# Loads split and placed one by one, an extra weight slot, the last inner blocks taken output by output, and one operand's differences on another engine

## The chip, the cores and the metric

The kernel runs on one core of a Trainium2 chip, in one launch. Times are device microseconds (us) of that core. Three timed runs of the kernel before gave 666.07, 663.64 and 663.92 us, median 663.92 us. Below, TensorE is PE in the rows (PEld is its weight load), VectorE is DVE, ScalarE is ACT, GpSimd is POOL, and SyncE's DMA queue is SP or SPq.

## The reference

Three stages follow each other: attention with a pooled part and a local part, a first MLP with a gate, and a second MLP of four experts, weighted by shares.

```
# attention, 2 batches, 8 heads, 576 tokens, 64 per head
q_d, k_d, v_d = (mean over groups of 4 tokens of q, k, v)
out_d = softmax(q_d k_d^T / 8) v_d            # repeated 4 times: out_up
scores = q k^T / 8, kept where |i - j| < 4
out_local = softmax(scores) v
x = out_up + out_local                         # 1152 tokens x 512
# first MLP
h = x @ w_in                                   # 512 -> 2048
g = h * clip(h + 3, 0, 6) / 6
x = g @ w_out                                  # 2048 -> 512
# second MLP
p = domain_probs / sum(domain_probs)
for e in range(4):
    out += p[:, e] * (relu(x @ w1[e]) @ w2[e]) # 512 -> 1024 -> 512
```

## The kernel before

**Attention** runs over eight units (a batch and a pair of heads), numbered by `t` in the loop at line 969. In its turn a unit gets its pooled scores, its mask and its local scores on TensorE, and the softmax on VectorE, ScalarE and GpSimd. In the same turn the unit before it is transposed (L627), and the one two back gets its values (L717, L728). All engines but SyncE keep the order in which the code is written; the queue of loads on SyncE is ordered by a scheduler, which puts a load as early as its slot allows. To hold a load to a place in the program, the code writes one element of its target on VectorE first (L171, L404): the load then comes behind that write. The keys and queries of units 6 and 7 (`load_qk(3)`), the first w_in block (`load_to(0)`) and the values of the second batch (`load_v(1, ..)`) are loaded in turns 1 to 3.

**First MLP.** w_in and w_out come as eight blocks each of 64-bit floats; each is loaded into one slot and turned into a high and a low float by `converting()`, a generator of steps on ScalarE and VectorE (L221, L231, L245, L254, L205, L210). Each product is three matmuls: high by high, high by low, low by high (`three`, L360 to L362). `first` computes h by 16 inner blocks `f` and three token chunks `c`; the gate is written at L790. After each, `convert(1)` takes a step if more than two slots are unused. The second half multiplies the gates by w_out: for each chunk it runs over 16 inner blocks and for each block over four outputs `dt`, with four banks (`accs`) open; after the last block ScalarE copies them to `x2` (L863). A slot is given back by `done_with`.

**Second MLP.** Each `r` is half an expert. The products with w1 use a scheme of seven block products in place of eight, and for it x is kept in two halves of 576 tokens, each as seven blocks: four own and the differences T1 to T4, high and low of each. `blocks_of_x2` makes them: GpSimd subtracts (`sub2`, L284), ScalarE writes the high part (L290) and VectorE the low (L295). Half 0 is made during the last chunk of the first MLP; half 1 in the first `r` (`xop1`), while TensorE works on half 0. A `Unit2` is one quarter of the inner size by one half of the tokens: `open`, `middle` and `close` are 12, 18 and 12 matmuls (L875), with sums on VectorE (L415, called `u` and `c`), Relu on ScalarE (L904) and the low part on VectorE (L907). In the first `r` the first two units need half 0 alone. From line 1134 on VectorE, ScalarE and GpSimd keep the order of the code. The shares are computed ahead of the loop (L1142 to L1147), from a load of 18 KB.

Of the kernel before, what the change touches and what calls it, by code (L numbers as in the profile page):

```python
# [82 lines left out]


# [29 lines left out]
def model(ctx: ExitStack, tc: tile.TileContext, qT, kT, v, dp, w_in, w_out, w1, w2, out):  # L114
# [60 lines left out]
    def converting():  # L175
# [42 lines left out]
        for i in range(2 * NW):  # L218
# [23 lines left out]
            elif i == 0:  # L242
                load_to(1)
# [123 lines left out]
    def load_qk(pair, units=(0, 1)):  # L367

        b, hp = divmod(2 * pair + units[0], NHP)
        if pair not in k_slots:  # L370
            k_slots[pair], q_slots[pair] = take(), take()
        n = len(units)
        at = units[0]
        k, q = k_slots[pair][0], q_slots[pair][0]
        k = k[:, at * SK : (at + n) * SK].rearrange("p (u s) -> p u s", u=n)
        for edge in (slice(0, FACTOR - 1), slice(SK - FACTOR + 1, SK)):
            nc.gpsimd.memset(k[:, :, edge], 0.0)
        nc.sync.dma_start(out=k[:, :, FACTOR - 1 : FACTOR - 1 + S], in_=kT[b, :, hp : hp + n])
        q = q[:, at * S : (at + n) * S].rearrange("p (u s c) -> p s u c", u=n, s=2)
        for s in range(2):  # L380
            nc.sync.dma_start(out=q[:, s], in_=qT[b, s, :, hp : hp + n, :])

# [10 lines left out]
    def load_v(b, p):  # L393
        v_slots.setdefault(b, []).append(take())
        slot, o = v_slots[b][p][0], FACTOR - 1
        if p == 0:
            nc.vector.memset(slot[:o, :DM], 0.0)
            v_rows(b, p, o, 0, WR, 0, 1)
            v_rows(b, p, WP, WP - o, WP, 0, 1)
            v_rows(b, p, 0, QB - o, P, 1, 2)  # L400
            v_rows(b, p, 0, 4 * QB - o, P, 2, 4)
        elif p == 1:
            if b:
                nc.vector.memset(slot[:1, :1], 0.0)  # L404
            v_rows(b, p, 0, 8 * QB - o, P, 0, 2)
            v_rows(b, p, 0, 12 * QB - o, P, 2, 4)
# [51 lines left out]
    load_qk(0, (0,))  # L458
    load_qk(0, (1,))
# [334 lines left out]
    def split_gate(c, f):  # L794
        g = hp_.tile([P, 2, TC], F32R, tag="h", name="h", bufs=NF2)
# [21 lines left out]
    def blocks_of_x2(s, x):  # L817

# [5 lines left out]
        room = x2_pair(s, 0)[:, 2 * PAIR : 3 * PAIR].rearrange("p (k n) -> p k n", k=2)  # L824
# [410 lines left out]
```

## Time and profile before

| | |
|---|---|
| timed runs, median | 663.92 us (663.64 to 666.07) |
| profiled execution, own time | 666.61 us |
| its span, first to last instruction | 664.9 us |
| mean granted TensorE clock | 0.992 |
| TensorE busy | 649.1 us (98%) |
| VectorE, ScalarE, GpSimd busy | 416.6, 253.6, 102.1 us |
| the chain that ended last | TensorE 89%, VectorE 6%, DMA 2% |

Read it so: TensorE is the engine with almost no idle time, and the chain of work that ended last lies on it. The rest is in three places that the 40 slices of the page show: slices 2 and 3 (from 16.6 us), slice 13 (from 199 us) and slice 18 (from 282 us). In the first and the last of them the granted clock is below full, too. VectorE is full in slices 5 to 7, 11 and 12.

### The profile page before, as it was taken

How to read it: one execution, taken by the hardware profiler on the slowest of the kernel's cores; microseconds unless marked ns; L12 is line 12 of the kernel's file. 1: busy time of each engine (PE TensorE's matmuls, PEld its weight loads, DVE VectorE, ACT ScalarE, POOL GpSimd, SP SyncE). 2: the span in 40 equal slices, each digit the busy share in tenths (PEclk: the TensorE clock that was granted, in tenths of full speed). 3: DMA queues.
4: the chain of work that ended last, by engine and by line, in shares of the span. 5: the costliest groups of instructions: out<-in, count | busy, mean ns of one | idle time of the engine just before them, and what ended most of it. 6: DMA issues, size and time to landing. Idle time of an engine off the chain costs nothing.

```text
span 664.9 us, 11951 instructions
## 1 busy us (share of the span) xinstructions
PE 649.1 (98%) x4929; PEld 584.3 (88%) x4943; DVE 416.6 (63%) x825; ACT 253.6 (38%) x591; POOL 102.1 (15%) x146
## 2 busy tenths in 40 slices
PE   7989999999999999989999999999999999999997
PEld 3556899999998999988898898898998998988985
DVE  5556799942598229296575575565665665765742
ACT  5536676542475236243133142233232241331310
POOL 4653100000000034060120211201201201201000
PEclk9979999999999999989999999999999999999999
DMA  8825233300350013200120110110110210300012
GB/s 279 278 69 190 82 111 127 127 1 0 127 191 1 0 64 102 90 1 1 38 90 0 64 65 1 63 64 1 65 64 0 68 61 0 123 5 1 1 48 96
DMA packets 11859, 45.89 MB, mean 69 GB/s; under 512 B 1302, under 2 KB 3350, under 8 KB 7708
## 3 DMA queue, kind: packets, MB, share of 16 engines
q1 hardware_dynamic: 11804, 45.12, 20.0%
q8 instruction: 39, 0.64, 0.4%
q14 instruction: 16, 0.13, 0.1%
HBM read 42.76 MB, written 2.36 MB: 68 GB/s over the span
## 4 chain that ended last, share of the span: by engine, by line
PE 89%; DVE 6%; DMA 2%; issue 1%; POOL 1%; SPq 1%; ACT 0%; POOLq 0%
PE bank L875 26%; PE bank L1120 10%; PE bank L1122 10%; PE bank L1121 10%; PE bank L362 9%; PE bank L360 8%; PE bank L361 8%; PE pair L717 2%; PE pair L524 2%; DVE slot L231 1%; PE pair L728 1%; DMA slot<-in_v_dram 1%; DMA slot<-in_qT_dram 1%; DVE slot L210 1%; DVE slot L254 1%
## 5 line engine op out<-in xcount | busy, mean ns | idle before, releaser
L875 PEld LDWEIGHTS bank<-xop,slot 128*128 128x128 f32 x1344 | 182.2, 189 | 3.8 <-DVE u L415 2.5
L875 PE MATMUL bank<-xop,slot 128*128 128x288 f32 x1344 | 183.5, 296 | 2.0 <-DVE u L415 2.0
L1120 PE MATMUL bank<-slot,h 128*128 128x512 f32 x288 | 113.5, 394 | 0.0
L1122 PE MATMUL bank<-slot,h 128*128 128x512 f32 x288 | 113.0, 392 | 0.0
L1121 PE MATMUL bank<-slot,h 128*128 128x512 f32 x288 | 111.9, 389 | 0.0
L1128 DVE SCALAR_TENSOR_TENSOR slot<-bank,pr,slot 128x512 f32<-128x512 f32 x63 | 47.3, 751 | 82.5 <-PE bank L1122 82.5
L415 POOL TENSOR_TENSOR st<-slot 128x256 f32<-128x256 f32 x16 | 13.2, 824 | 444.4 <-DMA slot<-in_w_dram 247.6
L362 PE MATMUL bank<-h,slot 128*128 128x384 f32 x192 | 65.0, 338 | 0.9 <-DVE slot L210 0.9
L360 PE MATMUL bank<-h,slot 128*128 128x384 f32 x192 | 64.9, 338 | 0.5 <-ACT slot L205 0.5
L1122 PEld LDWEIGHTS bank<-slot,h 128*128 128x128 f32 x288 | 54.1, 188 | 12.6
L361 PE MATMUL bank<-h,slot 128*128 128x384 f32 x192 | 64.7, 337 | 0.0
L1121 PEld LDWEIGHTS bank<-slot,h 128*128 128x128 f32 x288 | 54.1, 188 | 11.5
L1120 PEld LDWEIGHTS bank<-slot,h 128*128 128x128 f32 x288 | 54.1, 188 | 10.3
L360 PE MATMUL bank<-x,slot 128*128 128x384 f32 x188 | 63.1, 336 | 0.0
L362 PE MATMUL bank<-x,slot 128*128 128x384 f32 x188 | 62.9, 335 | 0.0
L361 PE MATMUL bank<-x,slot 128*128 128x384 f32 x188 | 62.9, 335 | 0.0
L415 DVE TENSOR_TENSOR u<-bank,u 128x288 f32<-128x288 f32 x96 | 43.5, 453 | 21.4 <-PE bank L875 21.1
L904 ACT ACTIVATE h<-c 128x288 fp32r<-128x288 f32 x64 | 27.9, 445 | 73.4 <-DVE c L415 73.3
L790 DVE SCALAR_TENSOR_TENSOR slot<-t,bank 128x384 f32<-128x384 f32 x47 | 25.8, 551 | 28.7 <-ACT t L789 28.4
L789 ACT ACTIVATE t<-bank,half__145 128x384 f32<-128x384 f32 x47 | 27.1, 581 | 41.9 <-PE bank L362 41.9
L290 ACT ACTIVATE slot<-st 128x512 fp32r<-128x512 f32 x32 | 19.2, 624 | 62.1 <-POOL st L284 62.1
L798 DVE TENSOR_TENSOR h<-slot,h 128x384 fp32r<-128x384 f32 x48 | 27.5, 582 | 22.2 <-ACT h L797 22.2
(115 smaller groups left out, 930.8 us busy)
## 6 DMA issues: line engine op xcount, KB each, us to landing
slot<-in_w_dram SPq DMA_DIRECT2D x16, 1024.0 KB, 4.8
slot<-in_w_in_dram SPq DMA_DIRECT2D x8, 1024.0 KB, 4.9
slot<-in_w_out_dram SPq DMA_DIRECT2D x8, 1024.0 KB, 4.8
slot<-in_v_dram SPq DMA_DIRECT2D x6, 512.0 KB, 9.3
out_dram<-slot SPq DMA_DIRECT2D x9, 256.0 KB, 2.0
slot<-in_kT_dram SPq DMA_DIRECT2D x3, 576.0 KB, 3.9
slot<-in_qT_dram SPq DMA_DIRECT2D x6, 288.0 KB, 5.5
slot<-in_kT_dram SPq DMA_DIRECT2D x2, 288.0 KB, 4.1
```

Source lines behind the costliest of these rows:

```text
L360: nc.tensor.matmul(ps, wh, xh, start=first, stop=False)
L361: nc.tensor.matmul(ps, wh, xl, start=False, stop=False)
L362: nc.tensor.matmul(ps, wl, xh, start=False, stop=last)
L415: eng.tensor_tensor(out=out, in0=a, in1=b, op=ALU.add)
L789: nc.scalar.activation(out=t, in_=ps, func=AF.Relu, bias=half_, scale=1.0 / (6.0 * UP))
L798: nc.vector.tensor_tensor(out=g[:, 1, :], in0=u, in1=r32(g[:, 0, :]), op=ALU.subtract)
L875: nc.tensor.matmul(ps, a[:, i, k], b[:, j, k], start=start and k == 0 and n == 0, stop=stop and k == 1 and n == 2, skip_group_check=True,)
L904: nc.scalar.activation(out=self.h[:, 0, i, j], in_=of, func=AF.Relu)
L1120: nc.tensor.matmul(ps, hh, w[:, 0], start=(f == 0), stop=False)
L1121: nc.tensor.matmul(ps, hh, w[:, 1], start=False, stop=False)
L1122: nc.tensor.matmul(ps, hl, w[:, 0], start=False, stop=(f == NF - 1))
L1128: nc.vector.scalar_tensor_tensor(out=to, in0=ps, scalar=share, in1=to, op0=ALU.mult, op1=ALU.add)
```

## The change

- **Loads of attention.** `load_next(t)` is called three times in every turn from 2 on, and each call issues one entry of the list `later`: the first w_in block in two halves, the values of batch 1 in four pieces, keys and queries of the last pair apart, the second w_in block in two halves. Most have a write of one element on VectorE ahead (`hold`). The steps of conversion begin in turn 3, with two.
- **First MLP.** A pool `late` with one more slot of weight size, from the end of attention on; the pool of split gates `h` has 7 buffers in place of 8; from inner block 11 on a step is taken if more than one slot is unused, in place of two.
- **Last inner blocks.** For the last chunk the last three blocks run output by output: for each `dt` all three blocks, then ScalarE's copy of that output.
- **Half 1 of x.** Its differences are six subtractions of 128x288 and one of twice that on VectorE, the first six ahead of the loop; high and low parts are spread over the first three units. The shares move behind the third unit.

```diff
+NL = 1
+NH = 7
+AHEAD = 2
+LAST = 3
...
-    SHORT = ("more", "slots", "mlp1")
-    LONG, FIRST = ("mlp1", "slots"), ("slots", "mlp1")
+    SHORT = ("more", "slots", "late", "mlp1")
+    LONG, FIRST = ("late", "mlp1", "slots"), ("slots", "late", "mlp1")
...
-            if i < 2:
-                nc.vector.memset(raw[i][0][:1, :1], 0.0)
             nc.sync.dma_start(out=raw[i][0].bitcast(I32), in_=sources[i])
...
+    def hold(part):
+
+        nc.vector.memset(part[:1, :1], 0.0)
+
+    def load_half(i, h):
+        if h == 0:
+            raw[i] = take(order=SHORT)
+            loaded[0] = i + 1
+        part = slice(h * WT, (h + 1) * WT)
+        hold(raw[i][0][:, part])
+        nc.sync.dma_start(out=raw[i][0].bitcast(I32)[:, part], in_=sources[i][:, part])
...
+        if b and p < 2:
+            hold(slot[:, 2 * DM * parts[0] :])
...
-        g = hp_.tile([P, 2, TC], F32R, tag="h", name="h", bufs=NF2)
+        g = hp_.tile([P, 2, TC], F32R, tag="h", name="h", bufs=NH)
...
+    def last_x2_sums():
+
+        b, t1, t2 = blocks_of_x2(1)
+        for k in (0, 1):
+            sub2(t1[:, k], b[0, 1][:, k], b[0, 0][:, k], nc.vector)
+        for k in (0, 1):
+            sub2(t2[:, k], b[1, 1][:, k], t1[:, k], nc.vector)
+            sub2(b[0, 1][:, k], b[1, 1][:, k], b[0, 1][:, k], nc.vector)
+
+    def last_x2(x):
+
+        b, t1, t2 = blocks_of_x2(1)
+        put = parts_of_x2(x)
+        yield from put(0, b[0, 0])
+        yield from put(1, t2)
+        yield from put(2, t1)
+        yield from put(3, b[0, 1])
+        yield from put(4, b[1, 0])
+        sub2(b[1, 0], b[1, 0], t2, nc.vector)
+        yield from put(5, b[1, 1])
+        yield from put(6, b[1, 0])
+        give_x2(1)
+
+    def second(c, fs, gs, accs):
+        for f in fs:
+            need(NW + f // 2)
         for dt in range(KD):
-            c0 = (f % 2) * DM + dt * P
...
+            for f, g in zip(fs, gs):
+                c0 = (f % 2) * DM + dt * P
+                three(
...
+            if f == NF1 - 1:
+                put_x2(c, dt, accs[dt])
...
+    later = [
+        lambda: load_half(0, 0),
+        lambda: load_half(0, 1),
+        lambda: load_v(1, 0, (0,)),
+        lambda: load_v(1, 0, (1,)),
+        lambda: load_v(1, 1, (0,)),
+        last_v,
+        lambda: load_k(NU // 2 - 1, held=True),
+        lambda: load_q(NU // 2 - 1, held=True),
+        lambda: load_half(1, 0),
+        lambda: load_half(1, 1),
+    ]
+
+    def load_next(t):
+        if t > 1 and later:
+            later.pop(0)()
...
+                load_next(t)
                 n.less_max()
-                if t == 2:
-                    load_v(1, 0)
-                elif t == 3:
-                    load_v(1, 1)
-                    load_v(1, 2)
...
             n.normalise()
+            load_next(t)
...
-        if t == 1:
-            load_to(0)
-        convert(3 if t >= NU else 1 if t > 1 else 0)
+        convert(3 if t >= NU else 2 if t == 3 else 1 if t > 3 else 0)
+        load_next(t)
...
-        if t == 3:
-            load_qk(3)
...
+    pools["late"] = tc.alloc_tile_pool(name="late", bufs=NL, side="right")
+    unused["late"] = NL
...
-            convert(1)
+            convert(1, 2 if f < 11 else 1)
...
-        second(c, f, ready.pop(0), accs)
+        if c < NTC - 1 or f < NF1 - LAST:
+            second(c, [f], [ready.pop(0)], accs)
+        elif f == NF1 - LAST:
+            second(c, range(f, NF1), ready, accs)
...
+    last_x2_sums()
...
-            order, steps = [(0, 0), (1, 0), (0, 1), (1, 1)], blocks_of_x2(1, xops[1])
+            order, steps = [(0, 0), (1, 0), (0, 1), (1, 1)], last_x2(xops[1])
...
-        run(steps, 2 if r == 0 else 0)
+        run(steps, 0 if r else 1)
...
             unit.open()
+            if r == 0:
+                run(steps, 1)
             if before:
                 before.close()
             unit.middle(before)
             before = unit
-            run(steps, 3 if r == 0 else 1)
-            if i == 1:
+            run(steps, (1, 2, 0, 0)[i] if r == 0 else 1)
+            if r == 0 and i == 2:
+                shares()
+            if i == (1 if r else 3):
                 for _ in steps:
                     pass
+            if i == 1:
                 load_out(r + 1)
```

The queue of loads on SyncE, from the queries of the last pair (slot_719 before, slot_782 after) to the values of batch 1, before:

```order
L381 DMA slot_719<-in_qT_dram 128x2x288 x2
L381 DMA slot_307<-in_qT_dram 128x2x288
L378 DMA slot_306<-in_kT_dram 128x2x576
L381 DMA slot_307<-in_qT_dram 128x2x288
L172 DMA slot_387<-in_w_in_dram 128x2048
L386 DMA slot_452<-in_v_dram 48x512
L386 DMA slot_452<-in_v_dram 64x512
L386 DMA slot_452<-in_v_dram 128x512
L386 DMA slot_452<-in_v_dram 128x2x512
L386 DMA slot_615<-in_v_dram 128x2x512
L386 DMA slot_619<-in_v_dram 48x512
L386 DMA slot_615<-in_v_dram 128x2x512
```

and after:

```order
L401 DMA slot_782<-in_qT_dram 128x2x288
L401 DMA slot_307<-in_qT_dram 128x2x288
L391 DMA slot_306<-in_kT_dram 128x2x576
L401 DMA slot_307<-in_qT_dram 128x2x288
L410 DMA slot_546<-in_v_dram 48x512
L189 DMA slot_445<-in_w_in_dram 128x1024
L410 DMA slot_546<-in_v_dram 64x512
L410 DMA slot_546<-in_v_dram 128x512
L189 DMA slot_445<-in_w_in_dram 128x1024
L410 DMA slot_546<-in_v_dram 128x2x512
L410 DMA slot_627<-in_v_dram 128x2x512 x2
L410 DMA slot_718<-in_v_dram 48x512
```

One half of the last pair's queries has moved behind all of these rows, the w_in block is in two, and both halves, and every values load of 128x2x512, now wait for a write on VectorE.

VectorE's row at the end of the first half of the first MLP, where L221 (L237 after) begins the conversion of a w_out block, L790 (L817) is a gate and L210 (L226) ends a conversion, before:

```order
L210 TENSOR_TENSOR slot<-slot 128x512 x3
L790 SCALAR_TENSOR_TENSOR slot<-t,bank 128x384
L210 TENSOR_TENSOR slot<-slot 128x512
L790 SCALAR_TENSOR_TENSOR slot<-t,bank 128x384 x15
L221 TENSOR_SCALAR slot<-slot 128x1024
```

and after:

```order
L226 TENSOR_TENSOR slot<-slot 128x512 x2
L817 SCALAR_TENSOR_TENSOR slot<-t,bank 128x384 x2
L237 TENSOR_SCALAR slot<-slot 128x1024
L259 TENSOR_SCALAR slot<-slot 128x1024
L247 SCALAR_TENSOR_TENSOR slot<-slot 128x512 x2
L817 SCALAR_TENSOR_TENSOR slot<-t,bank 128x384
L268 TENSOR_TENSOR slot<-slot 128x512 x2
L817 SCALAR_TENSOR_TENSOR slot<-t,bank 128x384
L226 TENSOR_TENSOR slot<-slot 128x512 x2
L817 SCALAR_TENSOR_TENSOR slot<-t,bank 128x384 x14
L237 TENSOR_SCALAR slot<-slot 128x1024
```

One whole conversion more stands ahead of the last gates; behind them five of the w_out blocks remain to be converted, where there were six.

VectorE's row at the start of the second MLP, where L295 (L309) is a low part of x, L415 (L442) the sums u and L907 (L968) the low part of h, before:

```order
L798 TENSOR_TENSOR h<-slot,h 128x384 x2
L1142 TENSOR_REDUCE psum__3358<-dps 128x9
L1143 TENSOR_SCALAR psum__3358<-psum__3358 128x9
L1145 RECIPROCAL prec<-psum__3358 128x9
L1147 TENSOR_TENSOR pr<-dps,prec 128x36
L295 TENSOR_TENSOR xop_3353<-slot,xop_3353 128x576 x2
L415 TENSOR_TENSOR u_3378<-bank,u_3378 128x288
L415 TENSOR_TENSOR u_3395<-bank,u_3378 128x288
L415 TENSOR_TENSOR u_3395<-bank,u_3395 128x288
L907 SCALAR_TENSOR_TENSOR h<-bank,h 128x288
L907 SCALAR_TENSOR_TENSOR h<-u_3395,h 128x288
L295 TENSOR_TENSOR xop_3353<-slot,xop_3353 128x576 x3
```

and after:

```order
L825 TENSOR_TENSOR h<-slot,h 128x384 x2
L298 TENSOR_TENSOR slot<-slot 128x288 x6
L309 TENSOR_TENSOR xop_3366<-slot,xop_3366 128x576
L442 TENSOR_TENSOR u_3386<-bank,u_3386 128x288
L309 TENSOR_TENSOR xop_3366<-slot,xop_3366 128x576
L442 TENSOR_TENSOR u_3405<-bank,u_3386 128x288
L442 TENSOR_TENSOR u_3405<-bank,u_3405 128x288
L968 SCALAR_TENSOR_TENSOR h<-bank,h 128x288
L968 SCALAR_TENSOR_TENSOR h<-u_3405,h 128x288
L309 TENSOR_TENSOR xop_3366<-slot,xop_3366 128x576
L442 TENSOR_TENSOR u_3434<-bank,u_3434 128x288
L309 TENSOR_TENSOR xop_3366<-slot,xop_3366 128x576
```

The subtractions (L298) have come here from GpSimd, the four rows of the shares have gone, and of the three low parts that stood in a row there is now one ahead of the next sum u.

## Rows read from the trace of the kernel before

**Rows 1.** Page, busy time of TensorE's instructions, and the queue q8 of section 3.
```profile
PE 649.1 (98%) x4929; PEld 584.3 (88%) x4943; DVE 416.6 (63%) x825; ACT 253.6 (38%) x591; POOL 102.1 (15%) x146
...
q8 instruction: 39, 0.64, 0.4%
```
**Rows 2.** Waits of TensorE, whole span: line, releaser, total us, times, longest.
```profile
PE pair L728 <- issue: 3.4, 1, 3.4
PE bank L875 <- DVE u L415: 2.0, 2, 1.5
...
PE bank L362 <- DVE slot L210: 0.9, 2, 0.5
```
**Rows 3.** Windows: stretch and us, busy (x count) per engine, PEclk, DMA share, GB/s.
```profile
20.70:27.44 6.74, 6.63 (x186) 4.51 (x189) 4.53 (x11) 3.17 (x14) 6.58 (x11) 1.00 0.84 288
27.44:40.26 12.82, 8.79 (x188) 5.48 (x189) 5.99 (x14) 6.34 (x20) 5.95 (x14) 0.77 0.66 195
40.26:47.47 7.21, 7.10 (x188) 4.87 (x189) 4.60 (x12) 3.03 (x13) 2.55 (x3) 0.93 0.15 59
...
34.43:41.26 6.83, 4.95 (x26) 2.81 (x26) 1.42 (x3) 1.56 (x4) 3.54 (x9) 0.50 0.34 108
```
**Rows 4.** Timeline of turn 3: start, us, instructions, idle before; restart and one-element write.
```profile
30.77 0.06 DVE L404 MEMSET slot<- 1x1 f32 x1
...
36.09 1.42 PE L728 MATMUL pair<-aTd,slot 80*64 80x144 f32 x7 [3.40 <-issue]
```
**Rows 5.** DMA of 22 to 34, of 27.8 to 33.4, of 33.4 to 34.7 us.
```profile
DMA packets 1766, 3.96 MB, mean 330 GB/s; under 512 B 153, under 2 KB 409, under 8 KB 1634
...
q1 hardware_dynamic: 899, 1.71, 101.7%
...
q8 instruction: 1, 0.02, 5.4%
```
**Rows 6.** Timeline of SyncE's queue: the loads of turns 1 to 3.
```profile
21.74 0.41 SPq L172 DMA_DIRECT2D slot<-in_w_in_dram  x1
22.20 9.92 SPq L386 DMA_DIRECT2D slot<-in_v_dram  x9
```
**Rows 7.** Windows in the first MLP's second half, and VectorE's timeline there.
```profile
200.00:220.00 20.00, 18.62 (x103) 17.34 (x102) 14.84 (x27) 9.18 (x18) 0.00 (x0) 1.00 0.00 1
220.00:240.00 20.00, 20.00 (x116) 20.00 (x115) 5.02 (x9) 5.20 (x10) 0.00 (x0) 1.00 0.13 40
196.00:210.00 14.00, 12.62 (x66) 11.04 (x65) 14.00 (x27) 6.66 (x13) 0.00 (x0) 1.00 0.03 14
...
175.91 0.69 DVE L221 TENSOR_SCALAR slot<-slot 128x1024 int32<-128x1024 int32 x1 [0.91 <-PE bank L362]
...
181.05 0.69 DVE L221 TENSOR_SCALAR slot<-slot 128x1024 int32<-128x1024 int32 x1
```
**Rows 8.** Start of the second MLP: timeline, chain (third row), L295 alone, and a window.
```profile
279.46 11.36 PE L875 MATMUL bank<-xop,slot 128*128 128x288 f32 x84
...
304.28 0.39 PE L1120 MATMUL bank<-slot,h 128*128 128x512 f32 x1
...
330.78 20.78 PE bank L875 x156
...
278.07 2.08 ACT L863 ACTIVATE slot<-bank 128x384 f32<-128x384 f32 x4 [11.07 <-PE bank L362]
...
282.10 6.91 POOL L284 TENSOR_TENSOR slot<-slot 128x576 f32<-128x576 f32 x4 [19.51 <-DVE xop L295]
...
286.24 4.60 DVE L295 TENSOR_TENSOR xop<-slot,xop 128x576 fp32r<-128x576 f32 x3 [0.44 <-ACT xop L290]
...
290.76 0.45 DVE L415 TENSOR_TENSOR u<-bank,u 128x288 f32<-128x288 f32 x1
...
L295 DVE TENSOR_TENSOR xop<-slot,xop x7: 750/759/1992, 281.3 to 295.6; 128x576 fp32r<-128x576 f32 x7
...
293.80:297.30 3.50, 3.39 (x14) 3.40 (x15) 3.24 (x8) 2.06 (x5) 0.00 (x0) 0.51 0.00 0
```

More of the change, by code (lines that the diff above doesn't have):

```diff
@@ L391, in v_rows, with load_v @@
         )
-    def load_v(b, p):
-        v_slots.setdefault(b, []).append(take())
+    def load_v(b, p, parts=(0, 1)):
+        if 0 in parts:
+            v_slots.setdefault(b, []).append(take())
         slot, o = v_slots[b][p][0], FACTOR - 1
+        if b and p < 2:
+            hold(slot[:, 2 * DM * parts[0] :])
         if p == 0:
[L397 to L401, printed above, removed]
+            if 0 in parts:
+                nc.vector.memset(slot[:o, :DM], 0.0)
+                v_rows(b, p, o, 0, WR, 0, 1)
+                v_rows(b, p, WP, WP - o, WP, 0, 1)
+                v_rows(b, p, 0, QB - o, P, 1, 2)
+            if 1 in parts:
+                v_rows(b, p, 0, 4 * QB - o, P, 2, 4)
         elif p == 1:
[L403 to L406, printed above, removed]
+            for n in parts:
+                v_rows(b, p, 0, (8 + 4 * n) * QB - o, P, 2 * n, 2 * n + 2)
         else:
@@ L823, in blocks_of_x2, with parts_of_x2, give_x2, first_x2 @@
                 b[c, h] = t[:, :, h]
-        room = x2_pair(s, 0)[:, 2 * PAIR : 3 * PAIR].rearrange("p (k n) -> p k n", k=2)
-        x = x.rearrange("p (b h k n) -> p b h k n", b=7, h=2, k=2)
-        def put(at, of):
-            return splits([(x[:, at, 0], x[:, at, 1], of)])
+        rooms = (
+            x2_pair(s, c)[:, 2 * PAIR : 3 * PAIR].rearrange("p (k n) -> p k n", k=2) for c in (0, 1)
+        )
+        return b, *rooms
+    def parts_of_x2(x):
+        x = x.rearrange("p (b h k n) -> p b h k n", b=7, h=2, k=2)
+        return lambda at, of: splits([(x[:, at, 0], x[:, at, 1], of)])
+    def give_x2(s):
+        for c in (0, 1):
+            give(x2_slots.pop((s, c)))
+    def first_x2(x):
+        b, room, _ = blocks_of_x2(0)
+        put = parts_of_x2(x)
         yield from put(0, b[0, 0])
@@ L840, in blocks_of_x2 @@
         yield from put(6, b[1, 0])
-        for c in (0, 1):
-            give(x2_slots.pop((s, c)))
-    def second(c, f, g, accs):
-        n = NW + f // 2
-        need(n)
-        for dt in range(KD):
-            c0 = (f % 2) * DM + dt * P
-            three(
-                accs[dt],
-                wt[n],
-                slice(c0, c0 + P),
-                (g[:, 0, :], g[:, 1, :]),
-                f == 0,
-                f == NF1 - 1,
-            )
-        if f < NF1 - 1:
-            return
-        for dt in range(KD):
-            for s, n0 in enumerate((0, PAIR)):
-                lo, hi = max(c * TC, n0), min((c + 1) * TC, n0 + PAIR)
-                if lo < hi:
-                    nc.scalar.activation(
-                        out=x2_at(s, dt)[:, lo - n0 : hi - n0],
-                        in_=accs[dt][:, lo - c * TC : hi - c * TC],
-                        func=AF.Copy,
-                        scale=1.0 / UP**2,
-                    )
+        give_x2(0)
@@ L871, in product, with put_x2 @@
+    def put_x2(c, dt, acc):
+        for s, n0 in enumerate((0, PAIR)):
+            lo, hi = max(c * TC, n0), min((c + 1) * TC, n0 + PAIR)
+            if lo < hi:
+                nc.scalar.activation(
+                    out=x2_at(s, dt)[:, lo - n0 : hi - n0],
+                    in_=acc[:, lo - c * TC : hi - c * TC],
+                    func=AF.Copy,
+                    scale=1.0 / UP**2,
+                )
     def product(ps, a, b, start, stop):
@@ L1099, in model @@
     hp_.release()
+    assert unused.pop("late") == NL
+    pools.pop("late").release()
     pools.pop("mlp1").release()
```

65 lines of the change are left out of this document (41 added, 24 removed).

## The prediction, made before the changed kernel ran

> **What bounds the kernel now.** First the page's busy times: TensorE is busy 649.1 of 664.9 us [rows 1], so a change that leaves its matmuls as they are, as this one does, can win only what TensorE waits and what it loses at the lower clock. Second, TensorE's waits: one of 3.4 us at L728 "for issue", that is for nothing the profile shows, two of 2.0 us together at L875 for a sum u on VectorE, and small ones at L362 for the last step of a conversion [rows 2]. Third, windows around each of the three, since a wait is not the whole price.
>
> Place A, turn 3 of attention. Turn 2 takes 6.74 us from one unit's first matmul to the next one's, turn 3 takes 12.82 and turn 4 takes 7.21 [rows 3]. That is 6.08 + 0.47 = 6.55 us lost: the 3.40 us of idle time ahead of the restart at 36.09 [rows 4], some smaller idle, and 6.83 us at a granted clock of 0.50 (1.2 GHz), which began while TensorE stood and in which its 4.95 us of work would have taken about half [rows 3].
>
> What did it wait for? Queue q8 moved 39 packets, 0.64 MB, in the whole execution [rows 1]: one packet for every 253 of TensorE's 9,872 instructions, so I read q8 as TensorE's program code. From 27.8 to 33.4 us q1, the loads, takes 101.7% of the DMA engines; the next packet of q8 runs within 33.4 to 34.7 [rows 5], and TensorE goes on some 1.4 us after it. So I read the idle as late code, behind the loads: 3.96 MB pass from 22 to 34 us at 330 GB/s [rows 5], most of them issued from 21.74 to 32.1 in one go [rows 6].
>
> Place B, second half of the first MLP. From 200 to 220 us TensorE does 103 matmuls, in the next 20 us 116 [rows 7]: 13 at 20/116 = 0.172 us each, 2.2 us lost. VectorE is busy 14.00 of 14 us there [rows 7]. It began the sixth last conversion at 175.91, after waiting for TensorE to give a slot back, and the next 5.14 us later [rows 7]; TensorE has done with one w_out block after two inner blocks of 12 matmuls, 24 x 0.172 = 4.1 us. VectorE falls behind by about 1 us with every block, and at the end TensorE waits for it.
>
> Place C, start of the second MLP. From the first L875 to the first L1120 it takes 304.28 - 279.46 = 24.82 us; the same 156 matmuls take 20.78 us in the next half expert [rows 8]. That is 4.04 us: the two waits for u (2.0), and a half clock stretch of 3.4 us behind them, 0.51 in the window from 293.80 [rows 8]. The u that TensorE waited for stands on VectorE behind three L295 that took 4.60 us from 286.24 [rows 8], because ScalarE had waited for GpSimd's four subtractions (6.91 us from 282.10), and because an L295 beside GpSimd's work takes 1.53 us where its median is 0.76 [rows 8].
>
> **The change part by part.** *Loads (A).* Nothing is removed; 4 MB are spread. The first w_in half waits on VectorE for the end of unit 2's pooled maximum, the second for its reciprocal, the third piece of values for unit 3's maximum, and so on, one entry at a time, three in a turn of 6.74 us. The first three pieces of values (480 KB) are not held, since the one element written lies outside their rows; they stay behind the w_in half in SyncE's queue. By the sizes in the code 576 + 288 + 96 + 512 + 384 + 512 KB = 2.4 MB are out before the middle of turn 3, where before 4 MB were. At 330 GB/s from 21.7 us they are through at about 29 us, so TensorE's packet, which must land about 1.4 us ahead of 32.7, finds free engines. I credit the whole 6.55 and charge 0.6 for what may remain: the next two packets each meet a piece of 512 KB, 1.6 us at that rate; the charge lies between 0 and one such piece.
>
> New waits of this part: on SyncE, behind each held load stand the next ones. On ScalarE and VectorE the first conversion in turn 3 waits for both w_in halves, with unit 4's softmax queued behind; the second half is issued in turn 2 and, by the rate above, lands early in turn 3, at whose end it is read. On GpSimd the sums of unit 6 wait for the last pair's queries, with the normalising of unit 5 behind; GpSimd is busy 2.55 of turn 4's 7.21 us [rows 3], so some 4 us of lateness stay hidden. Seven one-element writes at 0.06 us [rows 4] on VectorE, busy 4.53 of 6.74 us in a turn [rows 3], cost nothing.
>
> *Extra slot, fewer kept back, 7 buffers (B).* One conversion, 5.1 us of VectorE's time, moves into the last gates of the first half, where VectorE has room: it waits for TensorE at 175.91 [rows 7]. Five remain where there were six, so each is done 5.1 us earlier; the largest lag at the end is below 2.2 us. The wait goes, with 5.1 - 2.2 = 2.9 us to spare. Gates go two ahead as before, so one buffer less binds nothing. Credit 2.2.
>
> *Last blocks output by output, differences on VectorE (C).* TensorE's matmuls are the same; three outputs end 18, 12 and 6 matmuls earlier (3.1, 2.1 and 1.0 us at 0.172), the last one does not, and its copy still ends near 278.07 + 2.08 = 280.15 [rows 8]. Four of the six differences need not wait for that copy; two do. No row shows this subtraction on VectorE: half an L295 (0.38) and the u of the same 128x288 (0.45) [rows 8] are its bounds, and I take 0.45, nearest in shape. From 280.15 until the last low part is written VectorE has 2 + 9 + 6 such operations (differences, sums, low parts of h) and 7 + 1 of twice the size: 17 x 0.45 + 8 x 0.76 = 13.7 us, done by about 294. TensorE needs the first low part after 72 matmuls of 0.133 us, at 289.0, where it is done by 282, and the last after 132, at 297.0. GpSimd is silent there until the next weights' sums, so L295 stays at 0.76. The shares (four rows and a wait for their load) leave the head of VectorE's queue. If no wait is left, the clock has no cause to fall: credit 4.0, with 0 as the other end.
>
> **A rule against it.** The row shows one packet of q8 in 1.3 us after 5.6 us without one, then a restart [rows 5, 4]. The Trainium skill says in "Runtime: NRT & Kernel Launch", Instruction fetch mechanics, that the sequencer fetches the next page by itself and that this is mostly hidden in straight code; and in "DMA: Bandwidth & Descriptors", Queues, rings and completion order, that a DMA engine takes turns between queues, so that code would not wait behind all loads. By both, loads are not the cause, and A stays; that is the first rival. The trace speaks against it as far as one event can.
>
> **The sum.** 6.55 - 0.6 + 2.2 + 4.0 = 12.2 us. The profiled execution took 666.61 itself, so 654.4. It lies 2.7 us over the median of 663.92, and of three timed runs one took 666.07: either that difference goes along, which gives 651.7, or it is part of these very stalls, which gives 654.4. I take a value between: **652.8 us**.
>
> **The rivals.**
> 1. A stays: the pause is not late code, or the pieces still delay it. For: one event, "issue" names no cause. Against: the load queue at 101.7% until the packet came. 652.8 + 5.9 = 658.7.
> 2. C is only moved: VectorE, now with the differences, is late again at a unit of half 1, and most of the 4.04 us comes back. For: VectorE has 13.7 us of work in some 17. Against: 3 us to spare at the last part. About 652.8 + 3 = 656.
> 3. B stays, since conversions still start only when TensorE gives the slot back, and the freed time is lost to loads: 655.0.
> 4. Slower: spread loads put a piece in front of TensorE's code in each of turns 3, 4 and 5. One stall with its half clock costs 6.55 [rows 3]; three in place of one cost 13.1 more, less B and C (6.2): 663.9 + 6.9 = 671. It decides once a packet comes later than the code that TensorE still holds lasts; how long that is no row shows. Against: turns 4 and 5 carry some 1.2 MB each, 3.6 us of transfer in 6.74.
>
> **How the numbers follow.** All three places close: 0.57 (650 to 655). Rival 1: 0.15. Rival 2: 0.11. Rival 3: 0.09. Rival 4 and anything like it: 0.04. Two of rivals 1 to 3 together: 0.04, near 661. A measurement of this kernel can tell about 0.5% from no change, 3.3 us. Faster by more than that (below 660.6): 0.91; within: 0.05; slower: 0.04. The range reaches from 650.0, where all goes and the 2.7 us go along, to 658.5, which takes in rivals 2 and 3 and part of rival 1.
>
> **What would show it.** A right: turns 2, 3 and 4 each near 6.7 us, no idle for issue over 1 us, clock 1.00 from 20 to 60 us. Wrong: a wait for issue that remains, at L728 or elsewhere. B right: no wait at L362 or L360, some 116 matmuls in every 20 us. C right: about 20.8 us from the first L875 to the first L1120, L309 at 0.76 throughout, no wait for u. The prediction is wrong as a whole if TensorE's busy time itself changes, or if a new wait of more than 1 us stands in its list.

## The result, and the profile after

The changed kernel takes 657.33 us (median of 5 runs, 656.78 to 660.32), the kernel before 663.92 us: a ratio of 0.990, 95% interval 0.987 to 0.992. 652.8 was predicted, 650.0 to 658.5. The profiled execution after took 657.16 us (span 655.0, granted clock 1.00) where that of before took 666.61 (span 664.9), 9.45 us less; the sum of the prediction was 12.2.

The three places closed. The waits of TensorE after (line, releaser, total us, times, longest):

```profile
PE pair L551 <- DVE zeros L484: 1.3, 1, 1.3
PE pair L654 <- POOL ex L640: 0.7, 1, 0.7
PE pair L670 <- DVE slot L580: 0.4, 1, 0.4
PE pair L670 <- POOL slot L442: 0.4, 1, 0.4
PE pair L551 <- issue: 0.2, 1, 0.2
```

Those of [rows 2] are gone. The windows after that answer to [rows 3] (turns 2, 3 and 4 of attention) and [rows 7] (second half of the first MLP), with the same columns:

```profile
19.88:26.62 6.74, 6.63 (x187) 4.51 (x189) 4.11 (x14) 3.10 (x13) 6.58 (x11) 1.00 0.85 255
26.62:33.71 7.09, 6.96 (x187) 4.70 (x188) 5.34 (x15) 4.10 (x16) 4.26 (x8) 1.00 0.60 203
33.71:40.46 6.75, 6.64 (x188) 4.52 (x189) 5.73 (x17) 5.30 (x18) 3.97 (x9) 1.00 0.79 256
200.00:220.00 20.00, 20.00 (x115) 20.00 (x114) 6.54 (x11) 7.69 (x16) 0.00 (x0) 1.00 0.02 4
220.00:240.00 20.00, 20.00 (x116) 20.00 (x115) 5.17 (x9) 6.71 (x18) 4.57 (x5) 1.00 0.28 103
```

Turn 3 takes 7.09 us where it took 12.82, the DMA share falls to 0.60 there and rises in turn 4, the clock stays at 1.00, and in the MLP 115 matmuls stand where 103 stood. At the start of the second MLP (timeline of TensorE after: start, us, group) the first 156 L936 run without a break, so that the first L1204 follows 20.79 us after the first L936 (24.82 before, [rows 8]):

```profile
270.32 20.95 PE L936 MATMUL bank<-xop,slot 128*128 128x288 f32 x156
...
293.90 1.76 PE L936 MATMUL bank<-xop,slot 128*128 128x288 f32 x12
...
317.89 20.96 PE L936 MATMUL bank<-xop,slot 128*128 128x288 f32 x156
```

But the last two of these rows show what nobody had listed. From 293.90 to 317.89, 12 L936 and 96 matmuls of L1204 to L1206, it takes 23.99 us. The same rows of before are 23.57 apart:

```profile
307.05 1.75 PE L875 MATMUL bank<-xop,slot 128*128 128x288 f32 x12
...
330.62 4.55 PE L875 MATMUL bank<-xop,slot 128*128 128x288 f32 x33
```

No wait, no lower clock: each of the L1204 to L1206 starts 0.2333 us after the last one in place of 0.2291, on average, in all eight half experts. The page's groups of these three lines (instructions, busy us, mean ns) hint at it, before and then after:

```profile
L1120 PE MATMUL bank<-slot,h 128*128 128x512 f32 x288 | 113.5, 394 | 0.0
L1122 PE MATMUL bank<-slot,h 128*128 128x512 f32 x288 | 113.0, 392 | 0.0
L1121 PE MATMUL bank<-slot,h 128*128 128x512 f32 x288 | 111.9, 389 | 0.0
```

```profile
L1205 PE MATMUL bank<-slot,h 128*128 128x512 f32 x288 | 113.9, 395 | 0.0
L1206 PE MATMUL bank<-slot,h 128*128 128x512 f32 x288 | 113.9, 395 | 0.0
L1204 PE MATMUL bank<-slot,h 128*128 128x512 f32 x288 | 113.8, 395 | 0.0
```

The whole span by the starts of the stages' first matmuls, in us:

| stage | before | after | difference |
|---|---|---|---|
| to the first L360 (L374) | 70.18 | 63.47 | -6.71 |
| from there to the first L875 (L936) | 209.28 | 206.85 | -2.43 |
| first L875 (L936) to first L1120 (L1204) | 24.82 | 20.79 | -4.03 |
| from there to the last L1122 (L1206) | 355.95 | 359.66 | +3.71 |
| the rest | 4.67 | 4.23 | -0.44 |

So A, B and C gave 13.2 us, and 3.7 went again in a stage that the change was said not to touch. What does touch it: the shares are now computed behind the third unit, and with them two small tiles are allocated behind h instead of ahead of it. By the addresses in the two built programs this moved the tiles h, the weights of L1204 to L1206, 128 bytes down in SBUF.

### The profile page after: what moved, and what is told of

Same layout as the page of the kernel before. It is cut to its first block, busy times and chain, and to the rows that moved or that the text cites. A ratio compares the mean times of both kernels' runs of the same rounds, so it can differ in the third digit from the quotient of the medians.

```text
span 655.0 us, 11972 instructions
## 1 busy us (share of the span) xinstructions
PE 647.4 (99%) x4929; PEld 582.6 (89%) x4943; DVE 415.9 (63%) x839; ACT 253.3 (39%) x591; POOL 95.3 (15%) x142
## 4 chain that ended last, share of the span: by engine, by line
PE 96%; DMA 2%; SPq 1%; issue 0%; POOL 0%; DVE 0%; POOLq 0%
PE bank L936 27%; PE bank L1205 10%; PE bank L1206 10%; PE bank L1204 10%; PE bank L374 10%; PE bank L376 10%; PE bank L375 10%; PE pair L744 2%; PE pair L551 1%; DMA slot<-in_qT_dram 1%; PE pair L755 1%; DMA slot<-in_v_dram 1%; PE pair L607 1%; PE pair L724 1%; PE pair L670 1%; PE pair L654 1%
## 5 line engine op out<-in xcount | busy, mean ns | idle before, releaser
L936 PEld LDWEIGHTS bank<-xop,slot 128*128 128x128 f32 x1344 | 180.9, 188 | 1.3
L936 PE MATMUL bank<-xop,slot 128*128 128x288 f32 x1344 | 181.8, 295 | 0.0
L1206 PE MATMUL bank<-slot,h 128*128 128x512 f32 x288 | 113.9, 395 | 0.0
L1204 PE MATMUL bank<-slot,h 128*128 128x512 f32 x288 | 113.8, 395 | 0.0
L442 POOL TENSOR_TENSOR st<-slot 128x256 f32<-128x256 f32 x16 | 13.9, 868 | 467.4 <-DMA slot<-in_w_dram 220.5
L1206 PEld LDWEIGHTS bank<-slot,h 128*128 128x128 f32 x288 | 54.1, 188 | 13.0
L1204 PEld LDWEIGHTS bank<-slot,h 128*128 128x128 f32 x288 | 54.1, 188 | 12.3
L374 PE MATMUL bank<-h,slot 128*128 128x384 f32 x192 | 64.7, 337 | 0.0
L374 PE MATMUL bank<-x,slot 128*128 128x384 f32 x188 | 63.1, 336 | 0.0
L442 DVE TENSOR_TENSOR u<-bank,u 128x288 f32<-128x288 f32 x96 | 43.6, 454 | 20.4 <-PE bank L936 20.0
L817 DVE SCALAR_TENSOR_TENSOR slot<-t,bank 128x384 f32<-128x384 f32 x47 | 25.8, 552 | 24.5 <-ACT t L816 24.3
```

Of the source, the lines that this page charges most:

```text
L374: nc.tensor.matmul(ps, wh, xh, start=first, stop=False)
L442: eng.tensor_tensor(out=out, in0=a, in1=b, op=ALU.add)
L936: nc.tensor.matmul(ps, a[:, i, k], b[:, j, k], start=start and k == 0 and n == 0, stop=stop and k == 1 and n == 2, skip_group_check=True,)
L1204: nc.tensor.matmul(ps, hh, w[:, 0], start=(f == 0), stop=False)
L1206: nc.tensor.matmul(ps, hl, w[:, 0], start=False, stop=(f == NF - 1))
```

## The experiments

Each kernel is the changed one but for the edit named; medians stand against 657.33, stages against the table above. Beside these runs the kernel before took 663.76 to 664.61 us, so a difference of under 1 us between two medians shows nothing by itself; where one is read below, it is read from the stages of the traces.

### Is it the place of h?

**h_up.**

```diff
+    psum_ = work["pool"].tile([P, NTT], F32, name="psum_")
+    prec = work["pool"].tile([P, NTT], F32, name="prec")
     pr = work["pool"].tile([P, NTT, E], F32, name="pr")
     def shares():
-        psum_ = work["pool"].tile([P, NTT], F32, name="psum_")
...
-        prec = work["pool"].tile([P, NTT], F32, name="prec")
```

> The changed kernel with one edit: two small tiles of the shares are allocated ahead of the loop again, as before, so that the tiles h of the second MLP lie 128 bytes higher, where they lay before; no instruction is added or moved. In the changed kernel the matmuls L1204 to L1206 (weights from h) start 0.2333 us apart, before 0.2287; 864 of them make 4.0 us. Theory: the place of h in SBUF sets that spacing. Then the spacing goes back to about 0.2287, a half expert from 23.99 to 23.57 us, and the time falls by some 3.8 us, from 657.3 to about 653.5. Rival: the spacing comes from something else (the order of the work beside it, or an execution's luck). Then 657.3 and 0.2333 stay.

Measured: 653.70 us (ratio to before 0.985, interval 0.983 to 0.988), spacing 0.2291, as the trace of before has it too (the 0.2287 of the expectation does not come out of that trace). Timeline, the same two rows:

```profile
294.13 1.75 PE L936 MATMUL bank<-xop,slot 128*128 128x288 f32 x12
...
317.70 20.95 PE L936 MATMUL bank<-xop,slot 128*128 128x288 f32 x156
```

23.57 us again. No instruction differs, so places alone cost 3.6 us. The sums u and c moved along with h here; the next two kernels separate them: in before_h_down u and c stay, in h_sweep h shifts within its own tiles.

**before_h_down.** The kernel before, with h 128 bytes lower; the two small tiles go to another pool.

```diff
-    psum_ = work["pool"].tile([P, NTT], F32, name="psum_")
+    psum_ = work["sums"].tile([P, NTT], F32, name="psum_")
...
-    prec = work["pool"].tile([P, NTT], F32, name="prec")
+    prec = work["sums"].tile([P, NTT], F32, name="prec")
...
+        if r == 0:
+            pad = work["pool"].tile([P, 32], F32, name="pad")
+            nc.gpsimd.memset(pad[:1, :1], 0.0)
```

> The kernel before with one edit: the tiles h of the second MLP lie 128 bytes lower, as in the changed kernel; xop1 and the tiles u and c stay where they were. Theory (place of h sets the spacing of L1120 to L1122): 0.2287 becomes 0.2333 us, a half expert 23.57 becomes 23.99, and the time 663.9 becomes about 667.7. Rival (something else of the change): 663.9 and 0.2287. Beside that, this is a second look at attention as it was before: by the theory of late code the wait for issue in turn 3 and a half clock stretch behind it are there again, of a length that may differ from the 3.4 and 6.83 us of [rows 2, 3], since it hangs on when one packet of q8 gets through; if it is shorter here, that is where the profile of before lay above its median.

Measured: 667.61 us beside 664.49 for the kernel before on the same chip (ratio 1.0055, interval 1.0036 to 1.0074), spacing 0.2333. The place acts in the old kernel as in the new one. And its look at attention, a second one at the old loads:

```profile
PE pair L728 <- issue: 1.8, 1, 1.8
```

The wait of turn 3 is there again, but 1.8 us long in place of 3.4, with 3.41 us at half clock in place of 6.83; the first MLP begins at 67.72 in place of 70.18. The profiled execution of before was a dear one, by 2.5 us in this stage, close to the 2.7 by which it lay over its median.

**h_sweep.**

```diff
-            work["pool"].tile([P, 2, 2, NT], F32R, tag="h", name="h", bufs=2) for _ in range(2)
+            work["pool"].tile([P, 4 * NT + 64], F32R, tag="h", name="h", bufs=2) for _ in range(2)
         ]
+        h = [t[:, 8 * r : 8 * r + 4 * NT].rearrange("p (a f n) -> p a f n", a=2, f=2) for t in h]
```

> The changed kernel with the tiles h made 256 bytes longer, and used from an offset of 32 bytes times the number of the half expert: the first byte of h modulo 256 is 96 in the first half expert (as in the changed kernel), then 128, 160, 192, 224 (as before), 0, 32, 64. Theory (place of h): the spacing of L1204 to L1206 differs from half expert to half expert, 0.2333 in the first and 0.2287 in the fifth; the others are unknown and lie, if only these two levels exist, at one of them. Rival (not the place, or a place that counts beyond 256 bytes): one spacing in all eight. The time follows as the mean of the eight: 653.5 to 657.5.

Measured: 656.32 us (one run). The mean distance from one start of L1204 to L1206 to the next, by half expert (the moving operand, in the slots, is at byte 32 modulo 256 in all of them):

| first byte of h modulo 256 | 96 | 128 | 160 | 192 | 224 | 0 | 32 | 64 |
|---|---|---|---|---|---|---|---|---|
| ns | 233.3 | 234.3 | 233.2 | 233.6 | 229.1 | 233.4 | 227.2 | 233.2 |

Two of eight places are better than the rest, and the change had moved h from the second best to one of the others.

### A: is it code that waits behind loads?

**loads_old.** Loads and conversion steps of attention as before the change (the diff of the first part, reversed).

> The changed kernel with the loads of attention and the steps of conversion there as before (the w_in block and the values of batch 1 in one go in turn 2, the rest in turn 3); all else as changed. Theory (TensorE's code waits behind the loads): a wait for issue of some us at the first values matmul of turn 3 (L755) is back, with a packet of q8 that comes only when q1's burst is over, and a half clock stretch behind it; +4 to +6.5 us, so 661.3 to 663.8. Rival (turn 3's pause came from something else that the change moved or from chance): no such wait, 657.3.

Measured: 662.44 us (660.14 to 663.46), +5.1. Timeline of turn 3, and the DMA queue of the loads from 27 to 32.5 us (packets, MB, share of 16 engines):

```profile
35.26 1.42 PE L759 MATMUL pair<-aTd,slot 80*64 80x144 f32 x7 [3.13 <-issue]
```

```profile
q1 hardware_dynamic: 907, 1.75, 103.1%
```

and the window behind it:

```profile
33.00:40.00 7.00, 4.52 (x24) 2.58 (x26) 1.97 (x5) 1.95 (x6) 4.25 (x9) 0.53 0.32 91
```

The wait is back at the same matmuls, and the half clock behind it (0.53 over these 7 us), with all else as changed. This says that the loads' order does it, not yet how.

**burst.**

```diff
+    filler = const.tile([P, 1, 256], F32, name="filler")
+    nc.gpsimd.memset(filler, 0.0)
+    def burst():
+        nc.vector.memset(filler[:1, 0, :1], 0.0)
+        for i in range(4):
+            to = spare.tile([P, 8, 256], F32, name=f"spare{i}")
+            nc.sync.dma_start(out=to, in_=filler.to_broadcast([P, 8, 256]))
...
                 load_next(t)
+                if t == 6:
+                    burst()
```

> The changed kernel with a load on the DMA engines that nothing needs: in turn 6 of attention, where the changed kernel has no wait for issue, 4 MB (four DMAs from a small tile to a spare place in DRAM) are issued at once on SyncE's queue, held by one write on VectorE. No instruction of TensorE is touched. Theory (TensorE's code waits behind saturated DMA engines): a wait for issue of 1 to 8 us appears on TensorE in turn 6 or early in turn 7, ended by a late packet of q8, and a half clock stretch behind it; +3 to +12 us, so 660 to 669. Rival (the wait in turn 3 belonged to turn 3's own work, or code is served between other packets): packets of q8 keep their distance of 3.5 to 5 us, no such wait, 657.3 to 658. A wait for DMA on TensorE would show that the burst delayed operands, and would tell neither apart.

Measured: 661.50 us (659.71 to 667.33), +4.2. Timeline of TensorE, and windows (columns as in [rows 3]):

```profile
59.77 0.94 PE L744 MATMUL pair<-aT,slot 38*64 38x32 f32 x49
62.50 0.76 PE L744 MATMUL pair<-aT,slot 38*64 38x32 f32 x23 [1.78 <-issue]
```

```profile
57.40:63.00 5.60, 3.82 (x160) 2.87 (x158) 3.91 (x10) 3.94 (x15) 1.93 (x2) 0.99 1.04 342
62.90:69.73 6.83, 6.83 (x46) 5.56 (x40) 2.18 (x4) 1.60 (x5) 0.00 (x0) 0.50 0.91 302
```

TensorE stops in the middle of a run of equal matmuls that wait for nothing, in a turn that never stopped before, and 6.83 us at half clock follow. By the DMA records, packets of q8 begin at 52.2, 60.1 and 68.1 us here, and at 54.0, 57.4 and 62.4 in the changed kernel; TensorE goes on 1.4 us after the one of 60.1 ends. That is late code, brought about by loads that nothing needs.

The stall of turn 3 can be followed to its packet in the same way. In the traces of all fourteen kernels the second of the eight values matmuls of turn 3 (L755; L728 before, L759 in loads_old) starts 1.2 to 1.5 us after the fourth packet of q8 ends. That packet ends at 34.6 us in before, 34.0 in loads_old and 33.1 in before_h_down; with the loads spread it ends at 29.2 to 31.1, at 30.0 in the changed kernel, where the matmul starts at 31.43. So the change gains its time by letting this packet through 3 to 5 us earlier, and keeps almost none to spare: with the loads spread, TensorE still waits at this matmul for 0.44 us in burst_late (row below), 0.23 in diffs_pool, 0.16 in hg_32 and 0.15 in c_old.

```profile
PE pair L755 <- issue: 0.4, 1, 0.4
```

**burst_late.** The same burst in the fourth half expert (`if r == 3: burst()` ahead of its loop).

> The changed kernel with the same 4 MB that nothing needs (four DMAs from a small tile to a spare place in DRAM) issued in the fourth half expert of the second MLP, not in turn 6. There TensorE needs a packet of q8 every 24 us, in attention every 3.5 to 5. Theory (a packet that comes late by less than TensorE's stock lasts costs nothing): the burst of some 12 us leaves no wait for issue, 657.3. Rival (any burst stalls TensorE): a wait for issue there and half clock, +2 to +6 us.

Measured: 657.13 us, no wait at the burst (its one wait for issue, the 0.4 us above, is in turn 3). A window, and the DMA queues from 413 to 428 us:

```profile
414.00:428.00 14.00, 14.00 (x107) 14.00 (x106) 10.23 (x23) 5.24 (x13) 3.44 (x4) 1.00 1.05 363
```

```profile
q1 hardware_dynamic: 4246, 5.14, 98.5%
q8 instruction: 1, 0.02, 0.4%
```

The DMA engines are as full as in attention, and the packet of code comes at 427.2 where it came at 423.9; TensorE never stops. Late code costs in attention, where packets of the changed kernel begin 3.4 to 7.5 us apart (from 24 to 68 us), not here, where one lasts 20 to 24.

The Trainium skill says in "Runtime: NRT & Kernel Launch", Instruction fetch mechanics, that the fetch of the next page is mostly hidden: burst_late agrees (3.3 us late, 0 lost), loads_old and burst don't (3.1 and 1.8 us of wait). The Trainium skill says in "DMA: Bandwidth & Descriptors", Queues, rings and completion order, that an engine takes turns between queues; in burst the packet of 60.1 does come while q1 goes on at 102.8% until 68.1, so code is late beside loads there, but not last.

### B and C, each undone

**slots_old.**

```diff
-NH = 7
+NH = 8
...
-    pools["late"] = tc.alloc_tile_pool(name="late", bufs=NL, side="right")
...
-            convert(1, 2 if f < 11 else 1)
+            convert(1)
```

> The changed kernel with part B alone undone: no extra slot, eight buffers for the split gates, a step of conversion only if more than two slots are unused. Theory (VectorE falls behind by one conversion): TensorE waits at L374 to L376 in the second half of the first MLP and its matmuls stand further apart from 200 to 220 us; that half takes about 2.2 us longer, so 659.5. Rival (B was paid by the loads or by the slack that A won, the extra slot does nothing): 657.3 and no such wait.

Measured: 659.87 us, +2.5; the second half of the first MLP takes 103.58 us where it took 101.28, 2.30 more. A wait and a window:

```profile
PE bank L376 <- DVE slot L226: 0.9, 2, 0.5
```

```profile
194.00:214.00 20.00, 18.81 (x104) 17.86 (x105) 13.68 (x25) 9.00 (x18) 0.00 (x0) 1.00 0.00 1
```

104 matmuls in 20 us again, where the kernel before had 103 in its own window [rows 7]. The loads as changed don't help it; B stands on its own.

**c_old.** h_up with LAST = 1, the old order of high and low parts with the differences on GpSimd, and the shares ahead (the diff of the fourth part, reversed).

> The kernel h_up with part C undone as a whole: only the last inner block output by output, the differences of half 1 on GpSimd, high and low parts and the shares where they were before. It is to be compared with h_up (653.7), since the shares ahead of the loop put h where it lies there. Theory: the two waits for u and the half clock stretch behind them are back, from the first L936 to the first L1204 it takes 24.8 in place of 20.8 us, and the time is about 657.7. Rival (C is worth less where nothing was late before it): part of the 4 us, down to 653.7.

Measured: 656.89 us (655.53 to 658.57), +3.2 to h_up. Timeline of TensorE:

```profile
269.94 11.35 PE L939 MATMUL bank<-xop,slot 128*128 128x288 f32 x84
282.75 1.06 PE L939 MATMUL bank<-xop,slot 128*128 128x288 f32 x6 [1.46 <-DVE u L442]
284.31 9.05 PE L939 MATMUL bank<-xop,slot 128*128 128x288 f32 x66 [0.50 <-DVE u L442]
293.20 0.39 PE L1207 MATMUL bank<-slot,h 128*128 128x512 f32 x1
```

Both waits are back, to 0.1 us as in [rows 2]; 23.26 us from the first L939 to the first L1207, so 2.5 of the 4.0. This execution shows no half clock stretch behind them (66 matmuls in 9.05 us, where 66 took 10.54 in before). The other 1.5 is that stretch: before and before_h_down have it, this execution has not.

**diffs_pool.**

```diff
-            sub2(t2[:, k], b[1, 1][:, k], t1[:, k], nc.vector)
+            sub2(t2[:, k], b[1, 1][:, k], t1[:, k], nc.gpsimd)
```

(and so for all seven)

> The changed kernel with one thing of part C undone: the seven subtractions of half 1 run on GpSimd, in their new places; the order of the high and low parts, the shares and the last blocks stay as changed. Theory (the engine is what counts: GpSimd's subtractions are slow and make L309 beside them slow): ScalarE waits for GpSimd, L309 beside it goes from 0.76 towards 1.5 us, and 1 to 4 us come back, so 658.3 to 661.3. Rival (spreading the parts over three units counts, the engine does not): 657.3, and 20.8 us from the first L936 to the first L1204.

Measured: 658.06 us, +0.7, which the medians can't tell from nothing; by the stage 0.90 us, 21.69 in place of 20.79 from the first L936 to the first L1204. Timeline of TensorE, and of GpSimd:

```profile
270.78 17.75 PE L936 MATMUL bank<-xop,slot 128*128 128x288 f32 x132
289.20 3.43 PE L936 MATMUL bank<-xop,slot 128*128 128x288 f32 x24 [0.67 <-DVE u L442]
```

```profile
282.82 1.82 POOL L298 TENSOR_TENSOR slot<-slot 128x576 f32<-128x576 f32 x1 [9.12 <-DVE xop L309]
```

One late wait, behind the one large subtraction (1.82 us, on VectorE 0.76), for which ScalarE waits 1.91 us. The engine is worth about a quarter of C.

**last1.** `LAST = 1`.

> The changed kernel with one thing of part C undone: only the last inner block runs output by output, as before, in place of the last three; the differences stay on VectorE. The first outputs are then ready 3.1, 2.1 and 1.0 us later, so the six subtractions begin about 3 us later. Theory (the slack of VectorE in the changed kernel covers it: its last low part of x is written at 284.7, and TensorE needs it 9 units' parts later): 657.3 and no wait at L936. Rival (these three microseconds are what C lives on): a wait for u at L936 of up to 3 us, 658 to 660.

Measured: 660.10 us (656.69 to 661.11), yet the profiled execution, the one of 656.69, has no wait at L936, and each of its stages is as long as after (20.79 us at C). The other three were 3.2 to 4.4 us longer at a mean clock of 0.994 to 0.997. One more kernel was to tell whether that belongs to the edit.

### Better places

**hg_32.** h and the split gates of the first MLP both at byte 32 modulo 256.

```diff
     pr = work["pool"].tile([P, NTT, E], F32, name="pr")
+    work["pool"].tile([P, 48], F32, name="pad0")
...
+        if r == 0:
+            work["pool"].tile([P, 16], F32, name="pad1")
...
     ready = [split_gate(*g) for g in gs[:AHEAD]]
+    hp_.tile([P, 48], F32, name="pad2")
```

> The changed kernel with tiles moved and no instruction changed: the tiles h of the second MLP start at byte 32 modulo 256 (the best of the eight places in h_sweep, 0.2272 us a matmul against 0.2333 where the change left them), and the seven split gates of the first MLP, which are the moving operand of L374 to L376 in its second half, start at 32 as well, in place of 224 (in the changed kernel these matmuls start 0.1767 us apart where their weights lie at 32, against 0.1742 where x, at 32, is the moving operand). Theory (the places of the two operands set the spacing): 864 x 6.1 ns = 5.3 us and about 432 x 2.5 ns = 1.1 us less, 650.9 us, below both kernels and below h_up (653.7); the second half of the first MLP takes 100.2 in place of 101.3 us. Rival for the second part (the difference between x and gates is not one of place): 652.0, with 101.3 us there.

Measured: 650.71 us (650.19 to 653.97; ratio to before 0.980, interval 0.977 to 0.982), 6.6 us below the changed kernel without one instruction changed. The spacing of L1204 to L1206 is 0.2272 in all half experts, and the second half of the first MLP takes 100.02 us where it took 101.28: the place of a moving operand counts as well. Its profiled execution (653.12) shows this in turn 3 of attention, in timeline and window:

```profile
32.47 0.85 PE L755 MATMUL pair<-aTd,slot 80*64 80x144 f32 x7 [0.16 <-issue]
```

```profile
33.35:36.76 3.41, 3.41 (x18) 2.02 (x20) 1.91 (x5) 2.44 (x6) 3.25 (x8) 0.50 0.54 163
```

A stretch at half clock that begins 0.9 us after a wait for issue of only 0.16 us, at the place of A.

**hg_last1.** hg_32 with `LAST = 1`.

> hg_32 with only the last inner block output by output (as in last1). In last1 the profile shows no wait at L936 and the same length of each stage as in the changed kernel, but three of its four timed runs were 3 to 4 us longer at a mean clock of 0.994 to 0.997, and its profiled one, the fourth, was not. Theory (the order of the last blocks costs nothing; those three had a half clock stretch somewhere that falls on any of these kernels now and then, as hg_32's own profile shows one of 3.41 us in turn 3 of attention): median 650.7, as hg_32, with runs of 653 to 654 among them. Rival (the later outputs bring TensorE near a wait at the start of the second MLP, and with it the half clock): median 653 to 654.

Measured: 650.79 us (649.89 to 652.30; ratio to before 0.980, interval 0.978 to 0.982). So the order of the last blocks is worth nothing measurable, and the long runs of last1 did not come again with the same edit; where their lost clock lay, no trace shows. The profiled execution here (652.30, the longest of the five) has a half clock stretch in turn 3 too. In its windows:

```profile
26.00:32.97 6.97, 6.85 (x188) 4.58 (x188) 5.11 (x15) 4.14 (x15) 4.13 (x8) 1.00 0.73 221
32.97:36.38 3.41, 3.19 (x18) 1.54 (x16) 2.18 (x6) 2.41 (x6) 3.11 (x8) 0.50 0.69 204
```

TensorE had not been idle for more than 0.06 us at once since 24 us; its one wait for issue there, 0.22 us, lies inside the stretch. The second values matmul starts 0.35 us after the first, but so it does in the changed kernel, whose clock stayed. So the clock fell with no wait in the profile ahead of it, and what brings on such a stretch of 3.41 us is open.

## Why the prediction was near, and where it failed

- **A, credit 6.55 less 0.6.** Right in mechanism: loads_old and burst show the cause, and all traces the packet. In size it is 6.71 between the two profiled executions and about 5.1 in the medians (loads_old), since the wait of before was 3.4 us long in one trace and 1.8 in another. The charge of 0.6 is about what turn 3 still has over 6.74 us (0.35). It was put down to the packets behind the late one ("the next two packets each meet a piece"); what is left is at the late one itself, 0.15 to 0.44 us in four kernels. Rivals 1 and 4 fell.
- **B, credit 2.2.** Right: 2.43 between the profiles; by slots_old 2.30 in the stage and 2.5 in the median. Rival 3 fell.
- **C, credit 4.0.** Right as a sum (4.03 between the profiles, 3.2 in the medians by c_old), and the parts can now be told apart: 2.5 of waits, 1.5 of clock, and by diffs_pool 0.9 us of it for the engine, by hg_last1 none for the last blocks. If these add up, most of C is left for the new order of the parts and the shares, which was not run alone. VectorE's count held: the last low part is written 14.4 us after the first L936, as the prediction has it (293.9 - 279.46). The subtraction at 0.45 us and L309 at 0.76 held (rows below: count, min, median, max ns, first and last start us). "GpSimd is silent there until the next weights' sums" did not: the sums ran from 266.95, so that two subtractions took 0.97 and 0.99 us beside them, which TensorE did not wait for. Rival 2 fell.

```profile
L309 DVE TENSOR_TENSOR xop<-slot,xop x7: 746/751/759, 271.8 to 284.0; 128x576 fp32r<-128x576 f32 x7
...
L298 DVE TENSOR_TENSOR slot<-slot x7: 446/460/987, 266.3 to 282.3; 128x288 f32<-128x288 f32 x6, 128x576 f32<-128x576 f32 x1
```

- **"TensorE's matmuls are the same."** This is the step that failed. They are the same in number, form and order, and 864 of them got 4.2 ns slower each, 3.6 of the 3.7 us that the stage lost, because one part of C moved the allocation of two tiles. The prediction read of the moved shares only that they "leave the head of VectorE's queue", and it let a change that leaves the matmuls alone move nothing but waits and lower clock; the distance between matmuls, a third term, it put at nothing without a look at where the operands lie. With h back in its place (h_up) the kernel takes 653.70, 0.9 from the forecast.
- **Its own sign.** "Wrong as a whole if TensorE's busy time itself changes": it did change, from 649.1 us [rows 1] to 647.4, and to 642.5 in h_up (rows of their pages below, after and h_up), so by that sign the prediction is wrong as a whole. The sign could not have held, since work at half clock counts as busy and some of that time goes with A and C; but most of the 4.9 us between the two rows below, 3.7, is the moved h seen in it.

```profile
PE 647.4 (99%) x4929; PEld 582.6 (89%) x4943; DVE 415.9 (63%) x839; ACT 253.3 (39%) x591; POOL 95.3 (15%) x142
...
PE 642.5 (99%) x4929; PEld 581.6 (89%) x4943; DVE 416.8 (64%) x839; ACT 253.1 (39%) x591; POOL 95.4 (15%) x142
```

- **Luck.** 657.33 lies inside 650.0 to 658.5, but that range was opened upwards for rivals 2 and 3 and part of rival 1, and none of them came. A loss of 3.6 us that nobody had priced took the room; the range held it by luck.
- **"If no wait is left, the clock has no cause to fall."** Not so everywhere: hg_last1 has 3.41 us at half clock with no wait on its profile ahead of it.
- **The frame.** A value between 651.7 and 654.4 was taken for whether the 2.7 us between profile and median of before would stay. By before_h_down's shorter stall they were mostly part of A's own, so the upper end was the nearer one: h_up's profiled execution and its median are 653.78 and 653.70.

## What to carry to other kernels

Loads that nobody needs soon can stop the engine with the densest code, since its instructions come through the same DMA engines: spread them, and look for "issue" waits with a load queue near 100% in front of them. When a diff moves an allocation, compare the start-to-start distance of the longest matmul group before and after, and try a small pad (64 and 192 bytes in hg_32): here the places were worth 6.6 us against the changed kernel, and all the moved work some 10. Where a wait goes, count the half clock behind it too, but as a cost that only some executions pay, and look how near the next wait is: at A the packet comes with almost no time to spare.

## What was not expected of the hardware

The distance between matmuls depends on where their operands lie in SBUF: 128x512 ones took 227.2 ns with weights at byte 32 modulo 256, 229.1 at 224, and 233.2 to 234.3 at the six other places tried, the moving operand being at 32. With the moving operand at 224 the 128x384 ones of the changed kernel took 176.7 ns where the weights lay at 32 and 173.3 where they lay at 224. With the moving operand at 32 it was 173.6 and 173.3 there, and 173.7 and 173.3 for the gates that hg_32 moved to 32 (distances of over 0.25 us, three with x, are left out). The 128x288 ones, their weights at 32, took 133.2 to 133.6 with the moving operand at 32 and at 160. Why is open; only offsets in steps of 32 bytes were tried.
